# Spreading the hidden-dimension products of a Fourier layer over the blocks of a round

## The chip, the cores and the metric

The kernel runs on one core of one Trainium2 chip. The metric is the device time of one execution in microseconds (us). Work is done by TensorE (matmul, PE in the profile, its weight loads PEld), VectorE (DVE), ScalarE (ACT) and GpSimd (POOL); SyncE (SP) issues the DMA transfers.

## The reference

Four layers, on x of 2048 rows (S) and 640 columns (D), all in float32:

```python
x = x + A(layernorm(x))      # Fourier layer
x = x + B(layernorm(x))      # attention, causal window of 256, 32 heads of 20
x = x + A(layernorm(x))
x = x + B(layernorm(x))
# A(x): a = x @ dft_hid_re.T;  b = x @ dft_hid_im.T
#       y = dft_seq_re @ a - dft_seq_im @ b
```

The change lies in the Fourier layers A and at their last block. Float32 accuracy is reached with pairs of float16 numbers, a high and a low part, and three matmuls for each product (high by high, high by low, low by high).

## The kernel before

**Two Fourier layers and two attentions in turn.** The function `spectral` is a Fourier layer. The rows are 16 tiles of 128 (`NT`). Its work has two halves.

- A *stage* (`z_stage(s)`, from `Hidden.stage`) multiplies row tile s, normalised and transposed, by the hidden Fourier matrices (`whid`). It has four products of 15 matmuls, each into one of two `pf` PSUM banks. ACT empties a bank (L254), DVE empties it again with a subtraction (L257), and seven sums of the four results, split in high and low parts, go into a `zc` tile (L250 on ACT, L251 on POOL). A stage is 60 matmuls.
- A *block* (`main_a`, `main_b`, `main_c` for a round r and a pair j of output tiles) multiplies the sequence Fourier matrix by the `zc` tiles of one round. Seven products of 12 matmuls replace eight, in Strassen's manner, so the coefficients are sums too: `take_c` has POOL form them (L478 to L481), ACT round them to a high part (L486), and DVE form the low part (L489). A block is 84 matmuls, into the banks x, y and z, of which there are two each. DVE adds six of the seven results (L512) to residual rows or to slices of a scratch tile `pf`, and POOL adds three more (L526, L536, L547).

Four row tiles (`RS`) make a round, so a layer has four rounds (r = 0 to 3) of eight blocks (`NJ`, j = 0 to 7). The block's result is kept in the residual rows `res`, loaded ahead of the block and stored behind it: to `accd` in rounds 0 to 2, to `x2d` in the last.

**Where the stages stand before.** The four stages of round 0 come first. Of the stages for round r + 1, the first follows block 6 of round r, the second block 7, and the third and fourth stand at the start of round r + 1, ahead of its block 0. So blocks 0 to 6 run with no stage between them, and up to four stages come close together at the boundary. `zc` tiles have four buffers, beside two large `early` buffers that hold the tiles with s % 8 < 2.

**Side work.** `tick()` is called after each product of a stage and of a block (four times a stage, seven times a block). It pops one pair of coefficient roundings and advances every generator in the list `side` by a step. In the first Fourier layer the generators are: the norm of a row tile (`side_norm`, 11 steps from its load to the split tile `xs`), its transposes (`turn_x`, with a number of steps to wait first; `turned_x` ends it at once), the maxima of the attention's weights (`b_max`, DVE, L618, from round 0, block 1) and their splitting (`b_split`, ACT and POOL, L660 to L663, from round 1, block 2). Before, the norms for the next round begin ahead of blocks 3 and 4 and behind the transposes of the first two stages. In the second Fourier layer the normalised, transposed tiles were stored by the attention before it, and `hidden.fetch(s)` loads one into a ring of two; it stands just ahead of its stage.

**The last block.** In round 3, two tiles of the next attention are already prepared (`finish`, `ahead`). Ahead of block 7 two stacks are filled for that attention (`fill_stack`, eight loads each, tile `ks`), and the two residual rows of block 7 are loaded behind them by `main_a`. The attention's weights (`Projections`) take the large buffer that held the Fourier weights, once the last stage is over.

**What sets the order.** Each engine works through its own queue, and all loads and stores of this part are on SP's queue. The order in the source is not kept to the letter: in the trace six matmuls of the next block (`x<-early,cc`, at 143.49 us) stand between two products of a stage. `issue_after` holds some instructions behind others by hand.

Of the kernel before, what the change touches and what calls it, by code (L numbers as in the profile page):

```python
# [11 lines left out]
F32 = mybir.dt.float32  # L12
F16 = mybir.dt.float16
I32 = mybir.dt.int32
AF = mybir.ActivationFunctionType
OP = mybir.AluOpType
AX = mybir.AxisListType

S, D, H, DH, P = 2048, 640, 32, 20, 128
NT = S // P  # L20
ND = D // P
HD = D // 2
RS = 4
NR = NT // RS
NJ = NT // 2
# [24 lines left out]
TURN_STEPS = 8  # L50
NORM_STEPS = (4, 9)
ROW_STEPS = 3
X_UP = 2.0 ** 10
C_UP = 2.0 ** 8
W_UP = 2.0 ** 13
# [6 lines left out]
def body(ctx: ExitStack, tc: tile.TileContext, x_in, cmat, whid, wqkv, wo, out):  # L62
    nc = tc.nc
# [139 lines left out]
    class Hidden:  # L203
# [21 lines left out]
        def stage(self, s, pool, new=new_f):  # L225

            w, xt = self.w, self.xt(s)
            if s % 8 < 2:
                zc = new_early()[:, :14 * HD].rearrange("p (m a d) -> p m a d", m=7, a=2)
            else:  # L230
                zc = pool.tile([P, 7, 2, HD], F16, tag="zc", name="zc", bufs=4)
            self.zc[s] = zc
            b11, b12, t1, t2, t3, t4 = (self.zf[:, k] for k in range(6))
            z = None

            def product(c, n):
                nonlocal z
                z = new()
                cs = slice(n * HD, (n + 1) * HD)
                k = 0  # L240
                for dt in range(ND):
                    for l, r in ((0, 0), (0, 1), (1, 0)):
                        self.last = matmul(z[:, :HD], xt[:, l, dt], w[:, r, c, dt, cs],
                                                     start=k == 0, stop=k == 14).ins
                        k += 1
                        yield 136
                z = z[:, :HD]

            def parts(m, f):
                nc.scalar.activation(zc[:, m, 0], f, AF.Copy)  # L250
                nc.gpsimd.tensor_tensor(zc[:, m, 1], f, zc[:, m, 0], op=OP.subtract)  # L251

            def scaled(o):
                nc.scalar.activation(o, z, AF.Copy, scale=Z_DOWN)  # L254

            def minus(o, f):
                nc.vector.scalar_tensor_tensor(o, z, Z_DOWN, f, op0=OP.mult, op1=OP.subtract)  # L257

            yield from product(0, 0)
            scaled(zc[:, B11, 0])  # L260
            scaled(b11)
            minus(zc[:, B11, 1], zc[:, B11, 0])
            yield 0
            yield from product(0, 1)
            scaled(b12)
            minus(t1, b11)
            parts(T1, t1)
            yield 0
            yield from product(1, 1)
            scaled(zc[:, B22, 0])  # L270
            minus(t2, t1)
            minus(t3, b12)
            minus(zc[:, B22, 1], zc[:, B22, 0])
            parts(T2, t2)
            parts(T3, t3)
            yield 0
            yield from product(1, 0)
            scaled(zc[:, B21, 0])
            minus(zc[:, B21, 1], zc[:, B21, 0])
            minus(t4, t2)  # L280
            parts(T4, t4)
            yield 0
# [62 lines left out]
    def spectral(layer, res_src, hidden, first):  # L345
        with ExitStack() as st:
# [110 lines left out]
            def z_stage(s):  # L457
                for ns in hidden.stage(s, sb, spare if first and s < RS else new_f):
                    if ns == 0:
                        tick()  # L460
# [50 lines left out]
            def add(o, z, f):  # L511
                marks["dve"] = nc.vector.scalar_tensor_tensor(o, z, Y_DOWN, f, op0=OP.mult, op1=OP.add).ins  # L512
# [1 line left out]
            def new_bank(name):  # L514
                return pxy.tile([P, 512], F32, tag=name, name=name, bufs=2)

            def main_a(r, j):
                res = [keep.tile([P, D], F32, tag="res", name="res", bufs=4) for k in range(2)]
                for k in range(2):
                    load(res[k], res_src[2 * j + k] if r == 0 else acc_d[2 * j + k])  # L520
                f = sb.tile([P, 3, HD], F32, tag="pf", name="pf", bufs=2)
                x = new_bank("x")
                cc = CC.pop((r, j))
                z = product(r, x, cc, 0, True, False)
                marks["act"] = nc.scalar.activation(f[:, 0], z, AF.Copy, scale=Y_DOWN).ins
                nc.gpsimd.tensor_tensor(res[1][:, lo], res[1][:, lo], f[:, 0], op=OP.add)  # L526
                tick()
                state[r, j] = [res, f, cc, x]

            def main_b(r, j):  # L530
                (x0, x1), f, cc, x = state[r, j]
                p1, u2, u3 = (f[:, k] for k in range(3))
                y = new_bank("y")
                z = product(r, y, cc, 1, True, False)
                add(u2, z, p1)
                nc.gpsimd.tensor_tensor(x0[:, hi], x0[:, hi], u2, op=OP.add)  # L536
                tick()
                z = product(r, x, cc, 2, False, True)
                add(x0[:, lo], z, x0[:, lo])
                tick()  # L540
                zb = new_bank("z")
                z = product(r, zb, cc, 4, True, False)
                add(x1[:, hi], z, x1[:, hi])
                tick()
                z = product(r, y, cc, 3, False, False)
                add(u3, z, p1)
                nc.gpsimd.tensor_tensor(x1[:, hi], x1[:, hi], u3, op=OP.add)  # L547
                tick()
                state[r, j] = [(x0, x1), cc, y, zb]

# [121 lines left out]
            def keep_w():  # L672
                for k in range(2):
                    load(w_d[k], w[:, k].rearrange("p a b c -> p (a b c)"))
                    yield 1

            if first:
                constants()
                x = [load_x(s) for s in range(2)]
                f = [load_w(n) for n in range(NXIN - 2)]  # L680
                norm_x(0, x[:1], nc.vector)
                for n in range(10):
                    split_w(n, f[n])
                    if n == 1:
                        turn_x(0)
                        turned_x(0)
                        norm_x(1, x[1:], nc.gpsimd)
                    if n == 7:
                        x = [load_x(s) for s in range(2, 4)]
                    if n + NXIN - 2 < 10:  # L690
                        f.append(load_w(n + NXIN - 2))
            else:
                side.append(hidden.rest)
            load_c(0)
            for r in range(NR):
                for k in range(0 if r == 0 else 2, RS):
                    s = RS * r + k
                    if first:
                        if s == 1:
                            norm_x(2, x, nc.gpsimd)  # L700
                            marks["dve"] = normed[0]
                        if s:
                            turned_x(s)
                        if k < RS - 1:
                            turn_x(s + 1, 2)
                    elif s > 1:
                        hidden.fetch(s)
                    if r == 0 and k == 1:
                        load_c(1)
                        with behind() as order:  # L710
                            if not first:
                                order.enter_context(tc.issue_after(hidden.after))
                            take_c(0)
                    if first or s > 1:
                        z_stage(s)
                if r == NR - 1:
                    proj = Projections()
                for j in range(NJ):
# [9 lines left out]
                    if r == NR - 1 and j == NJ - 1:  # L728
                        for _ in early_qk:
                            pass  # L730
                        for k in (1, 0):
                            proj.stack[k] = new_stack()
                            fill_stack(proj.stack[k], 0, k)
                    if first:
                        if r < NR - 1 and j in (3, 4):
                            side.append(side_norm(RS * (r + 1) + j - 3))
                        if r < NR - 1 and j == 5:
                            turn_x(RS * (r + 1))
                    if j == 0 and r == 0:
                        with behind():  # L740
                            while splits:
# [4 lines left out]
                    with ExitStack() as order:  # L746
# [3 lines left out]
                        if j:  # L750
                            main_c(r, j - 1)
                        main_b(r, j)
                    if r < NR - 1 and j >= NJ - 2:
                        k = j - (NJ - 2)
                        s = RS * (r + 1) + k
                        if first:
                            turned_x(s)
                            turn_x(s + 1, 2 if k == 0 else 0)
                            side.append(side_norm(s + 2))
                        else:  # L760
                            hidden.fetch(s)
                        z_stage(s)
                main_c(r, NJ - 1)
                if r == NR - 1:
                    drain()
# [542 lines left out]
```

## Time and profile before

| | |
|---|---|
| runs | 2230.16, 2236.23, 2237.89 us |
| median of the runs | 2236.23 us |
| profiled execution, span from first to last instruction | 2233.0 us |
| median of the runs less that span | 3.2 us |
| PE, DVE, POOL, ACT busy | 2122.0, 1646.4, 1391.6, 1288.8 us |
| mean granted TensorE clock | 0.991 |

The profiled execution is told by its span; its time with what lies around the span is not listed apart, so the median stands for it. In a row of the timeline the first number is the start from the beginning of the span, the second the length, `x15` the number of instructions merged, and the brackets hold the engine's idle time before it and what ended that. The first Fourier layer runs from the start to about 591 us, the second from about 1174 to 1686 us; its first two stages already run inside the attention ahead of it.

### The profile page before, as it was taken

Reading aid. Unit: us, or ns where it says so; the run is one execution under the profiler, and the core shown is the slowest. Engines: PE = TensorE matmul, PEld = TensorE weight load, DVE = VectorE, ACT = ScalarE, POOL = GpSimd, SP = SyncE. Lnnn points to the kernel's source line nnn. Section 1 sums busy time; section 2 is a strip of 40 time slices with the busy share of each in tenths; the row PEclk is TensorE's granted clock in tenths of the full one; section 3 lists DMA queues with packets and bytes.
Section 4 is the critical chain, followed back from the end, with each engine's and each line's share of the span. In section 5 each row is a group of like instructions: output and inputs, shape, how many; then the busy total and the mean of one; then the engine's idle time right before and its main releaser. Section 6 shows DMA issues by size and latency. Waiting matters only on the chain.

```text
span 2233.0 us, 55112 instructions
## 1 busy us (share of the span) xinstructions
PE 2122.0 (95%) x21985; PEld 1494.7 (67%) x21985; DVE 1646.4 (74%) x3577; ACT 1288.8 (58%) x2155; POOL 1391.6 (62%) x1788
## 2 busy tenths in 40 slices
PE   7999899899999999999899999999998999999998
PEld 4767566676666766677566777777675666677765
DVE  8887958767677887887858758585767777777664
ACT  5434455443467777777754443434434777777775
POOL 5775968758355665566446858586674555566443
PEclk9999999999999999999999999999999999999999
DMA  6664646455533422333424536364743323332231
GB/s 252 219 224 143 229 138 225 156 188 175 142 79 67 103 71 73 94 91 84 134 79 160 193 127 212 110 207 145 256 133 96 83 63 85 93 87 59 57 80 37
DMA packets 187607, 292.96 MB, mean 131 GB/s; under 512 B 13908, under 2 KB 120660, under 8 KB 178004
## 3 DMA queue, kind: packets, MB, share of 16 engines
q1 hardware_dynamic: 186772, 288.77, 42.1%
q8 instruction: 172, 2.82, 0.5%
q14 instruction: 87, 0.71, 0.1%
q10 hardware_dynamic: 576, 0.66, 0.1%
HBM read 202.51 MB, written 86.87 MB: 130 GB/s over the span
## 4 chain that ended last, share of the span: by engine, by line
PE 59%; DVE 12%; DMA 4%; issue 3%; POOL 2%; ACT 2%; SPq 1%; DVEq 0%; POOLq 0%; ACTq 0%
PE pf L115 24%; PE pv L115 8%; PE y L115 7%; PE sp L115 5%; PE x L115 5%; PE z L115 5%; PE tp L115 3%; DVE m L1062 3%; DVE sp L1058 2%; PE pt L115 2%; DVE cc L489 1%; DMA res<-accd 1%; DMA x2d<-res 1%; PE acc L115 1%; DMA qs<-qkd 1%
## 5 line engine op out<-in xcount | busy, mean ns | idle before, releaser
L115 PEld LDWEIGHTS <-cc 128*128 128x128 f16 x5376 | 525.1, 98 | 215.6 <-issue 10.6
L1106 ACT ACTIVATE ptq<-tp,shift,alpha 128x768 f32<-128x768 f32 (+2 forms) x512 | 486.2, 950 | 163.6 <-PE tp L115 155.6
L115 PEld LDWEIGHTS <-big 128*128 128x128 f16 x4320 | 408.5, 98 | 151.9 <-issue 40.5
L1062 DVE TENSOR_REDUCE m<-sp 128x2 f32<-128x512 f32 (+1 forms) x512 | 345.1, 674 | 16.8
L1058 DVE COPY_PREDICATED sp<-mask,sp 128x256 f32<-128x256 int32 x448 | 190.8, 426 | 188.2 <-PE sp L115 176.5
L115 PE MATMUL pf<-early,big 128*128 128x256 f16 x2400 | 313.9, 274 | 2.9 <-ACT early L401 2.5
L1111 POOL TENSOR_SCALAR_AFFINE_SELECT ptq<-ptq 128x512 f32<-128x512 f32 x224 | 145.5, 649 | 265.4 <-ACT ptq L1106 261.7
L486 ACT ACTIVATE cc<-cs 128x512 f16<-128x512 f32 x256 | 151.6, 623 | 254.6 <-POOL cs L478 124.1
L115 PE MATMUL y<-zc,cc 128*128 128x320 f16 x1728 | 263.8, 300 | 2.4 <-DVE pf L512 2.4
L115 PE MATMUL pf<-big 128*128 128x320 f16 x1680 | 245.6, 304 | 19.2 <-DVE zc L257 9.3
L489 DVE SCALAR_TENSOR_TENSOR cc<-cs,cc 128x512 f16<-128x512 f32 x256 | 255.2, 1012 | 9.9 <-ACT cc L486 9.7
L489 DVE SCALAR_TENSOR_TENSOR cc<-cq,cc 128x512 f16<-128x512 f32 x192 | 198.7, 1036 | 0.0
L1113 POOL TENSOR_SCALAR_AFFINE_SELECT ptq<-ptq 128x512 f32<-128x512 f32 x256 | 163.9, 640 | 43.1 <-ACT ptq L1106 43.1
L115 PE MATMUL pv<-ptq,v 128*32 128x128 f32 (+1 forms) x3840 | 183.7, 330 | 0.0
L115 PE MATMUL z<-zc,cc 128*128 128x320 f16 x1152 | 178.5, 299 | 2.0 <-ACT cc L486 1.0
L115 PE MATMUL x<-zc,cc 128*128 128x320 f16 x1152 | 179.7, 299 | 0.0
L115 PE MATMUL sp<-ks,qs 62*128 62x256 f16 (+1 forms) x1792 | 153.6, 248 | 20.8 <-DVE m L1062 18.6
L115 PE MATMUL pf<-big,early 128*128 128x320 f16 x960 | 162.3, 301 | 6.4 <-DVE x L883 6.4
L1083 ACT ACTIVATE qs<-pt 2x512 f16<-2x512 f16 x224 | 131.0, 585 | 42.7 <-PE pt L115 40.0
L115 PE MATMUL tp<-qs,ks 62*128 62x128 f16 x2688 | 150.1, 217 | 3.2 <-ACT ptq L1106 2.7
L115 PE MATMUL pf<-bo,ot 128*128 128x320 f16 x840 | 147.2, 302 | 3.3 <-DVE ot L956 2.8
L167 POOL TENSOR_TENSOR xs<-lny,xs 128x640 f16<-128x640 f32 x63 | 94.2, 1497 | 83.3 <-ACT xs L166 82.6
(144 smaller groups left out, 3525.3 us busy)
## 6 DMA issues: line engine op xcount, KB each, us to landing
cq<-in_cmat_dram SPq DMA_DIRECT2D x64, 1024.0 KB
accd<-res SPq DMA_DIRECT2D x96, 320.0 KB
res<-accd SPq DMA_DIRECT2D x96, 320.0 KB
x<-x2d SPq DMA_DIRECT2D x64, 320.0 KB
qkd<-early SPq DMA_DIRECT2D x160, 128.0 KB
ks<-qkd SPq DMA_DIRECT2D x108, 160.0 KB
qs<-qkd SPq DMA_DIRECT2D x84, 160.0 KB
x2d<-res SPq DMA_DIRECT2D x32, 320.0 KB
```

What stands on the lines that cost most here:

```text
L115: i = getattr(nc.tensor, what)(*args, **kw)
L167: eng.tensor_tensor(lo, y, hi, op=OP.subtract)
L486: nc.scalar.activation(cc[m][:, 0], f, AF.Copy, scale=C_UP)
L489: nc.vector.scalar_tensor_tensor(cc[m][:, 1], f, C_UP, cc[m][:, 0], op0=OP.mult, op1=OP.subtract)
L1058: nc.vector.copy_predicated(sp[:, :, 2 * P:3 * P], mask[:, None, :].to_broadcast([P, 2, P]), far)
L1062: topped[0] = nc.vector.tensor_reduce(TOP[g // 4][:, g % 4], sp[:, :, c0:3 * P], axis=AX.X, op=OP.max).ins
L1083: nc.scalar.activation(o, handed[n][rs].rearrange("r (i p) t -> r i p t", i=2), AF.Copy)
L1106: nc.scalar.activation(q[:, h:h + 2, a0 + first:a0 + 3], tp[:, :, first * P:3 * P].rearrange("p a (b c) -> p a b c", c=P), AF.Sigmoid, bia ...
L1111: nc.gpsimd.affine_select(out=q[:, :, a0], in_=q[:, :, a0], pattern=[[0, 4], [-1, P]], base=0, channel_multiplier=1, compare_op=OP.is_gt, ...
L1113: ins = nc.gpsimd.affine_select(out=q[:, :, a0 + 2], in_=q[:, :, a0 + 2], pattern=[[0, 4], [1, P]], base=0, channel_multiplier=-1, compare ...
```

## The change

- The stages of the next round stand behind blocks 2, 4, 5 and 6 in round 0, and behind blocks 1, 3, 5 and 6 in rounds 1 and 2 (`STAGES`). None is left at the start of a round but the first.
- In the first Fourier layer each stage's norm begins three blocks ahead of it (`starts`), which for the first stage of rounds 2 and 3 is in the round before; its transposes wait four steps from the block ahead of the stage, or two from the end of the previous stage's.
- In the second Fourier layer the fetch of tile s + 2 stands right behind stage s.
- `zc` gets six buffers instead of four. The room comes from a slice of the scratch tile `pf` (its third sum is written over the first) and from a smaller DMA scratch.
- The residual rows of the last block are loaded ahead of the two stacks.

```diff
+STAGES = ((2, 4, 5, 6), (1, 3, 5, 6), (1, 3, 5, 6))
...
-                zc = pool.tile([P, 7, 2, HD], F16, tag="zc", name="zc", bufs=4)
+                zc = pool.tile([P, 7, 2, HD], F16, tag="zc", name="zc", bufs=6)
...
+            RES = {}
+
+            def load_res(r, j):
                 res = [keep.tile([P, D], F32, tag="res", name="res", bufs=4) for k in range(2)]
                 for k in range(2):
                     load(res[k], res_src[2 * j + k] if r == 0 else acc_d[2 * j + k])
-                f = sb.tile([P, 3, HD], F32, tag="pf", name="pf", bufs=2)
+                return res
+
+            def main_a(r, j):
+                res = RES.pop((r, j), None) or load_res(r, j)
+                f = sb.tile([P, 2, HD], F32, tag="pf", name="pf", bufs=2)
...
-                add(u3, z, p1)
-                nc.gpsimd.tensor_tensor(x1[:, hi], x1[:, hi], u3, op=OP.add)
+                add(p1, z, p1)
+                nc.gpsimd.tensor_tensor(x1[:, hi], x1[:, hi], p1, op=OP.add)
...
+            def starts(k):
+                return [max(NJ * r + STAGES[r][k] - 3, k) for r in range(NR - 1)]
...
-                for k in range(0 if r == 0 else 2, RS):
+                for k in range(RS if r == 0 else 0):
...
                     if first or s > 1:
                         z_stage(s)
+                    if not first and s > 1:
+                        hidden.fetch(s + 2)
...
+                        RES[r, j] = load_res(r, j)
                         for k in (1, 0):
                             proj.stack[k] = new_stack()
                             fill_stack(proj.stack[k], 0, k)
                     if first:
-                        if r < NR - 1 and j in (3, 4):
-                            side.append(side_norm(RS * (r + 1) + j - 3))
-                        if r < NR - 1 and j == 5:
-                            turn_x(RS * (r + 1))
+                        for k in range(RS):
+                            if n in starts(k):
+                                side.append(side_norm(RS * (starts(k).index(n) + 1) + k))
+                        if r < NR - 1 and j == STAGES[r][0] - 1:
+                            turn_x(RS * (r + 1), 4)
...
-                    if r < NR - 1 and j >= NJ - 2:
-                        k = j - (NJ - 2)
+                    if r < NR - 1 and j in STAGES[r]:
+                        k = STAGES[r].index(j)
                         s = RS * (r + 1) + k
                         if first:
                             turned_x(s)
-                            turn_x(s + 1, 2 if k == 0 else 0)
-                            side.append(side_norm(s + 2))
-                        else:
-                            hidden.fetch(s)
+                            if k < RS - 1:
+                                turn_x(s + 1, 2)
                         z_stage(s)
+                        if not first and s + 2 < NT:
+                            hidden.fetch(s + 2)
...
-    nc = _bacc.Bacc("TRN2", target_bir_lowering=False, num_devices=1)
+    nc = _bacc.Bacc("TRN2", target_bir_lowering=False, num_devices=1, dynamic_dma_scratch_size=1024)
```

More of the change, by code (lines that the diff above doesn't have):

```diff
@@ L515, in new_bank @@
                 return pxy.tile([P, 512], F32, tag=name, name=name, bufs=2)
-            def main_a(r, j):
+            RES = {}
+            def load_res(r, j):
                 res = [keep.tile([P, D], F32, tag="res", name="res", bufs=4) for k in range(2)]
@@ L531, in main_b @@
                 (x0, x1), f, cc, x = state[r, j]
-                p1, u2, u3 = (f[:, k] for k in range(3))
+                p1, u2 = (f[:, k] for k in range(2))
                 y = new_bank("y")
```

## The prediction

> **What bounds the kernel now.** I read the page first, then a table of stretches of the two Fourier layers, then TensorE's timeline around the stretches that lose time, and last all engines around one such place.
>
> From the page:
>
> ```profile
> PE 2122.0 (95%) x21985; PEld 1494.7 (67%) x21985; DVE 1646.4 (74%) x3577; ACT 1288.8 (58%) x2155; POOL 1391.6 (62%) x1788
> ```
>
> TensorE is the bound, but a share over the whole span doesn't say where the missing time lies. So I cut the first Fourier layer (54 to 592 us) at the round boundaries, and set beside it two stretches of the second Fourier layer, which runs the same loop. The columns are the stretch, its length, busy time and instructions of PE, PEld, DVE, ACT and POOL, the granted TensorE clock and the DMA load:
>
> ```profile
> core 0: us, PE busy (x) PEld busy (x) DVE busy (x) ACT busy (x) POOL busy (x), PEclk, DMA share, GB/s
> 54.00:130.00 76.00, 74.45 (x553) 53.46 (x551) 67.83 (x116) 31.90 (x59) 60.26 (x46) 1.00 0.66 221
> 130.00:166.00 36.00, 32.12 (x235) 22.60 (x234) 28.14 (x56) 14.60 (x30) 25.80 (x21) 0.95 0.63 214
> 166.00:247.00 81.00, 79.88 (x595) 57.18 (x592) 63.39 (x128) 37.36 (x73) 54.31 (x45) 1.00 0.49 163
> 247.00:308.00 61.00, 50.35 (x355) 35.33 (x356) 43.77 (x71) 31.92 (x58) 54.07 (x41) 0.92 0.60 202
> 308.00:389.00 81.00, 80.48 (x599) 57.69 (x597) 62.59 (x114) 41.09 (x78) 58.49 (x48) 1.00 0.57 189
> 389.00:426.00 37.00, 28.68 (x195) 19.47 (x196) 29.85 (x41) 14.31 (x27) 34.02 (x25) 0.93 0.56 183
> ...
> 1206.00:1268.00 62.00, 62.00 (x463) 44.76 (x461) 54.53 (x74) 23.79 (x44) 53.60 (x39) 1.00 0.64 222
> 1268.00:1326.00 58.00, 57.89 (x427) 41.57 (x425) 30.82 (x58) 25.23 (x55) 34.56 (x34) 1.00 0.36 119
> ```
>
> Inside a round of the first layer PE is almost never idle (81.00 - 79.88 and 81.00 - 80.48). At the three boundaries it loses 3.88, 10.65 and 8.32 us, 22.85 in all, and the granted clock falls to 0.92 to 0.95. The second layer's boundary (1268 to 1326) loses 0.11 us. So what the spreading of the stages can win lies in the first layer alone, at three places. TensorE's timeline names the waits there (start, length, instruction, count, and in brackets the idle time before it and its releaser):
>
> ```profile
> 139.79 3.25 PE L115 MATMUL pf<-big 128*128 128x320 f16 x15 [2.61 <-DVE zc L257]
> ...
> 162.40 2.20 PE L115 MATMUL pf<-big 128*128 128x320 f16 x15 [1.27 <-DVE zc L257]
> ...
> 248.36 0.45 PE L115 MATMUL pf<-idh,xs 128*128 128x128 f16 x5 [2.48 <-POOL xs L167]
> ...
> 279.77 4.16 PE L115 MATMUL pf<-big 128*128 128x320 f16 x15 [7.32 <-DVE early L257]
> ...
> 285.16 2.20 PE L115 MATMUL pf<-big 128*128 128x320 f16 x15
> ...
> 303.74 3.35 PE L115 MATMUL pf<-big 128*128 128x320 f16 x15 [1.97 <-DVE early L257]
> ...
> 390.33 0.45 PE L115 MATMUL pf<-idh,xs 128*128 128x128 f16 x5 [1.85 <-POOL xs L167]
> ...
> 422.02 4.16 PE L115 MATMUL pf<-big 128*128 128x320 f16 x15 [5.26 <-DVE zc L257]
> ...
> 457.36 4.44 PE L115 MATMUL pf<-big 128*128 128x320 f16 x30 [0.19 <-DVE zc L257]
> ```
>
> Three kinds. Twice the transposes of the next rows wait for their norm (xs from POOL): 2.48 + 1.85 = 4.33 us. Three times the third product of the stage after block 6 waits until DVE has emptied a pf bank: 2.61 + 7.32 + 5.26 = 15.19 us. Three times a product of a later stage waits likewise: 1.27 + 1.97 + 0.19 = 3.43 us. After such waits 15 matmuls take 3.25, 4.16, 3.35 and 4.16 us, where the undisturbed 15 at 285.16 take 2.20: slow tails of 1.05 + 1.96 + 1.15 + 1.96 = 6.12 us. Together 29.07 us.
>
> Why DVE is late, from all engines ahead of the wait at 422:
>
> ```profile
> 414.95 1.15 ACT L486 ACTIVATE cc<-cs 128x512 f16<-128x512 f32 x2 [2.72 <-POOL cs L479]
> 415.00 1.60 POOL L481 TENSOR_TENSOR cs<-cq,cs 128x512 f32<-128x512 f32 x1
> 415.79 3.89 DVE L489 SCALAR_TENSOR_TENSOR cc<-cs,cc 128x512 f16<-128x512 f32 x3
> ...
> 417.69 0.42 ACT L254 ACTIVATE zc<-pf 128x320 f16<-128x320 f32 x1
> ...
> 421.49 0.48 DVE L257 SCALAR_TENSOR_TENSOR zc<-pf,zc 128x320 f16<-128x320 f32 x1
> ```
>
> The stage's first eviction stands on ACT behind the high parts of the next block's coefficients, which wait for POOL's sums, and on DVE behind their low parts (3.89 us for three). These engines lag behind PE when the stage comes, and two pf banks cover no more. The second layer has the same queues without the norms and the weight splitting:
>
> ```profile
> 1272.48 8.58 PE L115 MATMUL pf<-big 128*128 128x320 f16 x60
> 1276.29 0.48 DVE L257 SCALAR_TENSOR_TENSOR zc<-pf,zc 128x320 f16<-128x320 f32 x1
> ...
> 1281.09 0.32 SPq L175 DMA_DIRECT2D big<-xud  x1
> ...
> 1303.72 16.49 PE L115 MATMUL pf<-big 128*128 128x320 f16 x120
> ```
>
> There DVE frees the first bank at 1276.29 + 0.48 = 1276.77, and the third product is due at half of 8.58 us, about 1276.8: no stall, but no margin either. Two stages in a row there (120 matmuls, 16.49 us) run without a gap.
>
> **The change part by part.** Instruction counts on every engine stay: 12 stages, 12 norms, 12 row loads in the first layer, 14 fetches in the second. What moves is where they stand.
>
> *Transposes.* A norm takes 11 ticks (4 to load, 7 to work), a block gives 7 and a stage 4, and norms now begin three blocks ahead of their stage, with the transposes a block or more later. The 4.33 us go; cover is a whole block of 84 matmuls, and if it were gone the 4.33 come back. I take -4.3.
>
> *Later stages at the boundary.* With a main block between any two stages there are 7 products between their evictions, so the 3.43 us of waits go. -3.4. Their load on the queues doesn't vanish, and is counted in the next term.
>
> *The stage behind a run of blocks.* Before, 7 blocks run without a stage; after, at most 3 (7, 0, 1 or 0 to 2), then 2 or 1. What makes DVE, ACT and POOL late in the first layer (operations between 54 and 426 us, with count, busy time and mean ns; the last row is from the view of one source line and has min, median and max ns):
>
> ```profile
> L663 POOL TENSOR_TENSOR bst<-wst,bst 128x640 f16<-128x640 f32 x15 | 24.1, 1609 | 2.6 <-ACT bst L661 2.6
> L618 DVE TENSOR_REDUCE wmax<-wst 128x1 f32<-128x640 f32 x20 | 16.2, 808 | 0.7 <-DMA wst<-in_wo_dram 0.7
> L251 POOL TENSOR_TENSOR zc<-big,zc 128x320 f16<-128x320 f32 x28 | 22.3, 812 | 21.8 <-ACT zc L250 21.8
> L257 DVE SCALAR_TENSOR_TENSOR big<-pf,big 128x320 f32<-128x320 f32 x33 | 15.2, 482 | 16.6 <-ACT big L254 5.8 <-ACT zc L254 5.6 <-ACT early L254 5.2
> ...
> L489 DVE SCALAR_TENSOR_TENSOR cc<-cs,cc x92: 675/1102/1889, 60.9 to 418.3; 128x512 f16<-128x512 f32 x92
> ```
>
> The worst lag, 7.32 us over 7 blocks, is 1.05 a block. A stage gives time back: 60 matmuls are 8.2 us of PE (half of 16.49), against 8 DVE operations of 0.482 (3.9 us) and 4 on POOL of 0.812 (3.2 us), over 4 us each time. By that, runs of 3 blocks (3.1 us) are repaid before the next and all 15.19 us go. Against it: the extra work isn't even. The maxima of the weights (20 of 0.808) and all four norms of the first round now meet in blocks 0 to 3, and the split of the weights (15 of 1.609 on POOL) meets norms in both later rounds; and the second layer shows that base lag alone uses the cover up. If the lag is only paid in smaller portions, none of it goes. Ends -15.2 and 0; nothing is nearer to either, so half, -7.6.
>
> *Slow tails.* They hang on the stalls: ends -6.1 and 0, half is -3.1. The rows show a slow tail after a wait of 2.61 and 1.97 us too, not after 1.27. [...]
>
> *Last round.* It had two stages directly ahead of its block 0 and now has block 7 there. Waits of PE in it, first layer:
>
> ```profile
> 504.49 1.79 PE L115 MATMUL z<-zc,cc 128*128 128x320 f16 x12 [1.00 <-ACT cc L486]
> ...
> 506.89 3.42 PE L115 MATMUL y<-zc,cc 128*128 128x320 f16 x24 [0.61 <-DVE pf L512]
> ...
> 528.98 2.52 PE L115 MATMUL pf<-early,big 128*128 128x256 f16 x15 [2.52 <-ACT early L401]
> ```
>
> That is 4.13 us. Without the relief they may double; since the attention's weights can load once the last stage is over, now a block earlier, they may vanish. Ends -4.1 and +4.1 per layer; I take +1 each, +2 in both, since the run of blocks without a stage grows by one.
>
> *Residual rows of the last block.* Their two loads now stand ahead of sixteen stack loads on SP:
>
> ```profile
> 578.77 2.05 SPq L175 DMA_DIRECT2D res<-accd  x2
> ...
> 584.74 1.79 PE L115 MATMUL y<-zc,cc 128*128 128x320 f16 x12 [0.58 <-DVE pf L512]
> ...
> 587.49 0.86 POOL L536 TENSOR_TENSOR res<-res,pf 128x320 f32<-128x320 f32 x1 [14.00 <-DMA res<-accd]
> ...
> 588.78 1.79 PE L115 MATMUL z<-zc,cc 128*128 128x320 f16 x12 [0.21 <-DVE res L512]
> ```
>
> POOL waits 14.00 us for them, which looks large, but PE loses only 0.21 of it: the 0.58 at 584.74 is one product waiting for the bank that DVE just read, which the load doesn't touch. The stacks land about 2.05 us later; all are issued by 578.77 and first read when the attention starts, after the product at 588.78. So -0.2 per layer, -0.4 in both (ends -0.8 for the whole wait with what follows, and +2).
>
> *The rest at nothing.* The third pf slice goes because the last sum is written over p1; DVE's write waits for POOL's read of p1, which is three products older. If that cover were gone, one y bank would be held longer. The DMA issue list has SP's queues alone, so nothing in it shows a use of the smaller scratch. In the second layer the fetch at 1281.09 already leaves as the stage ends (1272.48 + 8.58 = 1281.06), more than 20 us ahead of the stage that needs it (1303.72): writing it behind the stage changes nothing, and SP's wait for that slot is there already, with PE never held.
>
> Sum: -4.3 - 3.4 - 7.6 - 3.1 + 2.0 - 0.4 = -16.8 us. The profiled execution spans 2233.0 us, so 2216.2; the median of the runs is 2236.2, 3.2 above that span, so 2219.4.
>
> **The rivals.**
>
> *All lags repaid.* The 15.2 and 6.1 go whole and the last round loses nothing: -4.3 - 3.4 - 15.2 - 6.1 - 0.4 = -29.4, 2206.8 us. For it: the balance of 4 us a stage against 1.05 a block. Against: bunched norms.
>
> *The lag is paid in portions, or the order hardly moves.* Every stage then waits a little, 15.2 and 6.1 stay: -4.3 - 3.4 + 2.0 - 0.4 = -6.1, 2230.1 us. For it: the second layer's margin of nothing.
>
> *Slower: each of the first layer's 12 stages finds DVE late.* The six waits for a pf bank average 18.62 / 6 = 3.1 us, with 6.12 / 6 = 1.0 of tail. Paid at all 12 stages that is 49 us in place of 24.7, so +24.7 - 4.3 + 2.0 - 0.4 = +22, 2258 us. It decides from a mean loss of 2.3 us a stage, at which the sum is zero. For it: the low part of a coefficient takes 675 ns at best and 1889 at worst, and stages now put POOL work beside twice as many of them. [...] Against: the second layer does it after block 6 with no stall.
>
> **How the numbers follow.** The forecast (2211 to 2227) gets 0.46, the full repayment 0.23, the portions 0.15, the slower case 0.16. Under 0.3% (6.7 us) a measurement of this kernel tells little, its three runs lying 7.7 us apart. So faster 0.69, same 0.15, slower 0.16. The range runs from just below the full repayment, 2204, to the lighter part of the slower case, 2240.
>
> **What would show it.** Right: in the first layer no transposes waiting for POOL xs, no wait over 4 us ahead of a stage's third product, granted clock near 1.00 at the boundaries; the second layer's Fourier loop unchanged within 2 us; POOL's 14 us wait for res gone with PE's end of block moved by a few tenths. Wrong: waits for DVE at most of the 12 stages, summing over 25 us; new gaps in the second layer's mid-round stages; or longer gaps in the last round.

## The result and the profile after

| | before | changed |
|---|---|---|
| median of six runs | 2232.52 us | 2217.49 us |
| lowest to highest | 2230.16 to 2237.89 | 2212.66 to 2221.21 |
| profiled execution, span | 2233.0 us | 2219.4 us |

The ratio is 0.9932, 95% interval 0.9917 to 0.9947: 15 us faster. The profiled execution of the changed kernel took 2221.21 us, 1.8 us more than its span, and was the slowest of its six.

The page of the changed kernel, the first line of its first part:

```profile
PE 2115.5 (95%) x21985; PEld 1493.1 (67%) x21985; DVE 1615.9 (73%) x3577; ACT 1283.3 (58%) x2155; POOL 1376.1 (62%) x1788
```

PE has the same 21985 instructions and 6.5 us less of busy time. The stretches of the first Fourier layer, of the first attention and of the second Fourier layer, with the columns as before (the granted clock is the third number from the end):

```profile
54.00:578.00 524.00, 498.20 (x3734) 360.00 (x3731) 382.19 (x734) 231.95 (x446) 380.70 (x330) 0.99 0.55 190
578.00:1163.00 585.00, 554.77 (x7256) 383.61 (x7255) 454.49 (x1182) 424.86 (x649) 320.94 (x566) 0.99 0.33 89
1163.00:1673.00 510.00, 502.88 (x3738) 363.15 (x3737) 341.42 (x588) 200.59 (x406) 353.05 (x314) 1.00 0.50 173
```

The first layer is counted here from its first block to the first product of the attention. For the kernel before the same count runs from 53.75 to 591.15:

```profile
54.00:592.00 538.00, 506.01 (x3740) 362.71 (x3738) 401.74 (x735) 235.68 (x447) 389.25 (x330) 0.98 0.56 185
```

So the first layer went from 537.4 to 524.4 us (53.74 to 578.11), 13.0 less; PE's idle time fell by some 6 us and its busy time by some 7, at a granted clock of 0.99 in place of 0.98. The first attention took 585.2 after 584.6, the second layer 509.7 after 509.9, the second attention 546.4 after 547.4. The gain lies in the first Fourier layer, as forecast. Its waits in the changed kernel, from TensorE's timeline:

```profile
74.45 0.45 PE L116 MATMUL pf<-idh,xs 128*128 128x128 f16 x5 [2.62 <-ACT xs L167]
...
94.46 2.20 PE L116 MATMUL pf<-big 128*128 128x320 f16 x15 [2.03 <-DVE zc L258]
...
98.90 2.20 PE L116 MATMUL pf<-big 128*128 128x320 f16 x15 [0.84 <-ACT big L402]
...
128.92 2.20 PE L116 MATMUL pf<-big 128*128 128x320 f16 x15 [1.74 <-DVE zc L258]
...
214.40 2.20 PE L116 MATMUL pf<-big 128*128 128x320 f16 x15 [1.45 <-DVE early L258]
...
241.93 1.79 PE L116 MATMUL y<-zc,cc 128*128 128x320 f16 x12 [1.24 <-DVE pf L513]
...
252.17 4.16 PE L116 MATMUL pf<-big 128*128 128x320 f16 x15 [4.38 <-DVE early L258]
...
308.22 4.37 PE L116 MATMUL pf<-big 128*128 128x320 f16 x30 [1.67 <-DVE zc L258]
...
354.98 3.20 PE L116 MATMUL pf<-big 128*128 128x320 f16 x15 [3.52 <-DVE zc L258]
...
389.76 2.20 PE L116 MATMUL pf<-big 128*128 128x320 f16 x15 [1.43 <-DVE zc L258]
```

The waits for a pf bank held by DVE are 2.03 + 1.74 + 1.45 + 4.38 + 1.67 + 3.52 + 1.43 = 16.22 us. They were 18.62, so almost all are still there. But they come in seven pieces with a maximum of 4.38 in place of 7.32, and only two have a slow tail (15 matmuls in 4.16 and 3.20, not 2.20). Last round and last block, same view:

```profile
494.89 1.79 PE L116 MATMUL z<-zc,cc 128*128 128x320 f16 x12 [1.04 <-ACT cc L487]
...
498.28 3.42 PE L116 MATMUL y<-zc,cc 128*128 128x320 f16 x24 [1.59 <-DVE pf L513]
...
512.00 0.45 PE L116 MATMUL pf<-idh,xs 128*128 128x128 f16 x5 [1.87 <-POOL xs L168]
...
572.72 1.79 PE L116 MATMUL z<-zc,cc 128*128 128x320 f16 x12
...
575.98 2.20 PE L116 MATMUL pf<-big,early 128*128 128x320 f16 x15
```

In the last round 1.04 + 1.59 + 1.87 = 4.50 us against 4.13 in the rows of before. At the block's end no product waits.

### The profile page after: what moved, and what is told of

It reads as the page before. It is cut to its first block, busy times and chain, and to the rows that moved or that the text cites. A ratio compares the mean times of both kernels' runs of the same rounds, so it can differ in the third digit from the quotient of the medians.

```text
span 2219.4 us, 55110 instructions
## 1 busy us (share of the span) xinstructions
PE 2115.5 (95%) x21985; PEld 1493.1 (67%) x21985; DVE 1615.9 (73%) x3577; ACT 1283.3 (58%) x2155; POOL 1376.1 (62%) x1788
## 4 chain that ended last, share of the span: by engine, by line
PE 72%; DVE 17%; issue 4%; DMA 3%; ACT 2%; POOL 2%; SPq 0%; DVEq 0%; POOLq 0%; ACTq 0%
PE pf L116 27%; PE y L116 11%; PE pv L116 8%; PE x L116 8%; PE z L116 7%; PE sp L116 5%; DVE cc L490 4%; PE tp L116 3%; DVE m L1076 3%; DVE sp L1072 2%; PE pt L116 2%; DMA res<-accd 1%; DVE lnt L141 1%; DMA qs<-qkd 1%; PE acc L116 1%
## 5 line engine op out<-in xcount | busy, mean ns | idle before, releaser
L116 PEld LDWEIGHTS <-cc 128*128 128x128 f16 x5376 | 524.4, 98 | 213.2 <-issue 10.0
L1076 DVE TENSOR_REDUCE m<-sp 128x2 f32<-128x512 f32 (+1 forms) x512 | 345.2, 674 | 16.8
L490 DVE SCALAR_TENSOR_TENSOR cc<-cs,cc 128x512 f16<-128x512 f32 x256 | 228.6, 901 | 0.0
L554 POOL TENSOR_TENSOR res<-res,pf 128x320 f32<-128x320 f32 x64 | 77.2, 1206 | 136.4 <-DVE pf L513 123.8
```

The source lines that it names most:

```text
L116: i = getattr(nc.tensor, what)(*args, **kw)
L490: nc.vector.scalar_tensor_tensor(cc[m][:, 1], f, C_UP, cc[m][:, 0], op0=OP.mult, op1=OP.subtract)
L554: nc.gpsimd.tensor_tensor(x1[:, hi], x1[:, hi], p1, op=OP.add)
L1076: topped[0] = nc.vector.tensor_reduce(TOP[g // 4][:, g % 4], sp[:, :, c0:3 * P], axis=AX.X, op=OP.max).ins
```

## The experiments

All ratios are to the kernel before on the same chip; its medians there were 2232.67, 2233.57 and 2232.95 us in the three sets of runs.

**The residual rows alone.** The kernel before, with

```diff
...
+                        RES[r, j] = load_res(r, j)
                         for k in (1, 0):
                             proj.stack[k] = new_stack()
...
```

> The kernel before with the last block's residual rows ahead of the stacks, and nothing else of the change. Theory: the two block ends, where PE waited 1.37 us in the first layer (565 to 592) and 1.16 us in the second (1660 to 1686), lose all of it, so about 2.5 us under the kernel before: 2230.0 beside 2232.5. Rival, the term as it was predicted: 0.4 us, 2232.1; the waits then stay in the trace and went with the moved stages.

Measured: 2227.55 us, ratio 0.9978 (0.9969 to 0.9987), 5 us less. The products at both block ends wait no more; the first layer took 534.7 us (2.7 less) and the second 508.0 (1.9 less). The theory holds for the waits, and the predicted 0.4 was too small: the waits of 0.58 us at each end, which I took to be untouched, went too. The time fell by about twice the 2.5 us that these waits come to (by 2.9 to 6.9, by the interval); where the rest comes from is not shown. The price that the prediction allowed for does show: one of the attention's first products waits 0.78 us for its stack (589.48), which it did not before.

**Without the residual rows.** The changed kernel less that line.

> The changed kernel with the residual rows behind the stacks again. Theory: POOL waits some 14 us for res again and PE loses 2.5 us at the two block ends: 2220.0 beside 2217.5. Rival: 0.4 us, 2217.9.

Measured: 2230.72 us, ratio 0.9994 (0.9983 to 1.0005): without this line the whole change wins nothing that can be told. Both theories fall. At the end of the first layer:

```profile
567.05 1.29 SPq L176 DMA_DIRECT2D res<-accd  x2
...
574.12 0.86 POOL L543 TENSOR_TENSOR res<-res,pf 128x320 f32<-128x320 f32 x1 [13.57 <-DMA res<-accd]
...
574.94 0.86 POOL L533 TENSOR_TENSOR res<-res,pf 128x320 f32<-128x320 f32 x1
575.41 3.36 PE L116 MATMUL z<-zc,cc 128*128 128x320 f16 x12 [4.24 <-DVE res L513]
575.83 0.49 DVE L513 SCALAR_TENSOR_TENSOR pf<-y,pf 128x320 f32<-128x320 f32 x1
...
578.56 3.13 PE L116 MATMUL y<-zc,cc 128*128 128x320 f16 x12
```

PE waits 4.24 us ahead of the z product, and its 12 matmuls then take 3.36 us in place of 1.79; in the second layer it is 4.35 and 3.36. The kernel before waited only 0.21 there, with the same late rows (POOL waited 14.00 us then, 13.57 now). The last lines show what is new. DVE writes its sum into pf (575.83) only behind POOL's addition at 574.94, which reads p1. POOL can't read p1 before the residual rows are there, DVE can't write over it before POOL has read it, and the y bank stays taken, so the y product stands behind the z product, at 578.56. In the kernel before, DVE wrote the third slice at 584.20 and let the y bank go while POOL still waited, so a y product (584.74) and 15 matmuls of the attention ran ahead of the z product at 588.78 and covered its wait:

```profile
584.20 0.49 DVE L512 SCALAR_TENSOR_TENSOR pf<-y,pf 128x320 f32<-128x320 f32 x1 [4.84 <-PE y L115]
...
586.37 2.20 PE L115 MATMUL pf<-big,early 128*128 128x320 f16 x15
```

The small edit, and not the moved stages, was the next suspect.

**The write over p1 alone.** The kernel before, with

```diff
...
-                p1, u2, u3 = (f[:, k] for k in range(3))
+                p1, u2 = (f[:, k] for k in range(2))
...
-                add(u3, z, p1)
-                nc.gpsimd.tensor_tensor(x1[:, hi], x1[:, hi], u3, op=OP.add)
+                add(p1, z, p1)
+                nc.gpsimd.tensor_tensor(x1[:, hi], x1[:, hi], p1, op=OP.add)
```

> The kernel before with the third sum written over p1 and two pf slices, nothing else of the change. Theory: at the last block POOL reads p1 only when the residual rows are there, so DVE can't write over it, the y bank stays taken and PE waits at both block ends, some 4 to 5 us each: 2241 beside 2232.5. Rival, as predicted: the write over p1 costs nothing, 2232.5.

Measured: 2241.69 us, ratio 1.0032 (1.0021 to 1.0043), 8 us slower. At the two block ends:

```profile
589.21 3.36 PE L115 MATMUL z<-zc,cc 128*128 128x320 f16 x12 [5.10 <-DVE res L512]
...
1686.48 3.21 PE L115 MATMUL z<-zc,cc 128*128 128x320 f16 x12 [5.18 <-DVE res L512]
```

These waits of 5.10 and 5.18 us and the slow matmuls behind them, less the waits that the kernel before had there, come to 10.7 us. In this profile the two Fourier layers took 5.8 and 5.3 us more than before, so the block ends account for the loss.

**Both small edits, no stage moved.** The two diffs above together.

> The kernel before with the write over p1 and the residual rows ahead: both small edits, no stage moved. Theory: the early rows give POOL its read of p1 in time, so the 8 us that the write over p1 costs alone go whole, and the time is that of the residual rows alone, 2227.5 beside 2232.7. Rival: the write over p1 costs by itself and the two add up, -5 + 8: 2236.

Measured: 2228.77 us, ratio 0.9984 (0.9970 to 0.9998). The cost of the write over p1 is gone once the rows are early, within what these intervals can tell, and no product waits at either block end. So the small edits are worth about 4 us together, and the moved stages, with their norms and the six `zc` buffers, bring the ratio from 0.9984 to 0.9932, about 11.5 us. The first layer took 536.7 us here and 524.4 in the changed kernel.

**The second layer alone.** The changed kernel, with the first layer's stages, norms and transposes in their old places:

```diff
...
-                    if r < NR - 1 and j in STAGES[r]:
-                        k = STAGES[r].index(j)
+                    at = (NJ - 2, NJ - 1) if first else STAGES[min(r, NR - 2)]
+                    if r < NR - 1 and j in at:
+                        k = at.index(j)
...
```

> The changed kernel with the first layer's stages, norms and transposes where they were before; the second layer's stages stay spread and the residual rows stay ahead. Theory: the second layer had no stalls to win back, so only the block ends remain, less up to 1.6 us in the second layer's last round: 2230 to 2232 beside 2232.5, with the first layer's stalls of 2.6, 7.3 and 5.3 us back. Rival: the second layer or the order of the attentions carries the gain, 2222 or less.

Measured: 2230.96 us, ratio 0.9992 (0.9981 to 1.0002). The first layer is back at 537.6 us, with waits of 2.62, 6.02 and 5.27 at the three stages. The theory holds. The six `zc` buffers are there in this run too, so they alone don't shorten the first layer. Norms and transposes move with their stages in every run here; what each is worth by itself is not told apart.

**The first layer alone.** The counterpart, the second layer's stages in their old places (its fetches stay as changed).

> The changed kernel with the second layer's stages where they were before, the first layer's spread. Theory: the second layer wins nothing by the spread and pays some 1.6 us in its last round, so this is 1 to 2 us under the changed kernel, 2215.5 to 2216.5. Rival: the spread pays in the second layer too, over 2219.

Measured: 2217.62 us, ratio 0.9940 (0.9924 to 0.9956), not to be told from the changed kernel. In its profile the second layer took 508.7 us against 509.7, and its last round waits 0.89 and 0.61 us where the changed kernel waits 1.05 and 1.59. The sign is the expected one; the size lies below what these runs resolve.

**More lag, before.** The kernel before with POOL's subtraction in the weight splitting made twice:

```diff
                     nc.gpsimd.tensor_tensor(lo, f, hi, op=OP.subtract)
+                    nc.gpsimd.tensor_tensor(lo, f, hi, op=OP.subtract)
```

> The kernel before with POOL's subtraction in the weight splitting (15 of 1.6 us, in rounds 1 and 2 of the first layer) made twice, the second time over the same result: 24 us more of POOL. Theory: this lag is paid at the stage behind the run of seven blocks, so the boundaries of rounds 1 and 2 lose more: 8 to 16 us slower, 2241 to 2249 beside 2232.5. Rival: POOL's lag doesn't set the stalls (DVE's own does): within 3 us of the kernel before.

Measured: 2257.14 us, ratio 1.0102 (1.0084 to 1.0120), 23.6 us slower: all of the added POOL time, more than expected.

```profile
254.68 0.72 PE L115 MATMUL pf<-idh,xs 128*128 128x128 f16 x5 [5.90 <-POOL xs L167]
...
278.99 1.79 PE L115 MATMUL y<-zc,cc 128*128 128x320 f16 x12 [3.00 <-DVE pf L512]
...
295.89 4.16 PE L115 MATMUL pf<-big 128*128 128x320 f16 x15 [11.04 <-DVE early L257]
...
322.01 3.78 PE L115 MATMUL pf<-big 128*128 128x320 f16 x15 [3.43 <-DVE early L257]
```

The wait at the stage behind the long run is 11.04 us (7.32 before), and the lag now shows ahead of it too, at the transposes (5.90) and a block's y bank (3.00).

**More lag, after.** The same doubling in the changed kernel.

> The changed kernel with the same doubled subtraction. Theory: each stage gives time back before the next, so the added 24 us of POOL cost the changed kernel less than half of what they cost the kernel before: 3 to 6 us, 2221 to 2224 beside 2217.5. Rival, the lag paid in portions: the same cost in both kernels, whatever its size.

Measured: 2224.04 us, ratio 0.9950 (0.9932 to 0.9968), 4 us by the ratios and 6.5 us by the medians more than the changed kernel. Its largest wait is 4.91 us (4.38 without the doubling):

```profile
253.54 4.16 PE L116 MATMUL pf<-big 128*128 128x320 f16 x15 [4.91 <-DVE early L258]
```

The same 24 us of work cost the kernel before some four to six times as much; in the profiles the first layer is 24.1 us longer there and 3.2 us here. So a stage between the blocks does let POOL catch up, and lag doesn't pile up over a round.

**Stages between blocks, but late.**

```diff
-STAGES = ((2, 4, 5, 6), (1, 3, 5, 6), (1, 3, 5, 6))
+STAGES = ((4, 5, 6, 7), (4, 5, 6, 7), (4, 5, 6, 7))
```

> The changed kernel with the stages behind blocks 4, 5, 6 and 7 of every round: none at the start of a round, but one run of four blocks (0 to 3) without a stage. Theory: what counts is that a main block stands between any two stages, and a run of four is little worse than one of three: 2216 to 2221 beside 2217.5. Rival: the even spread is what pays, and half of the first layer's 13 us comes back: 2224.

Measured: 2228.04 us, ratio 0.9966 (0.9955 to 0.9977). The rival holds: half of the gain or a little more is lost. In the profile the first layer took 531.5 us, against 524.4 in the changed kernel.

```profile
119.62 4.16 PE L116 MATMUL pf<-big 128*128 128x320 f16 x15 [4.62 <-DVE zc L258]
...
258.18 3.60 PE L116 MATMUL pf<-big 128*128 128x320 f16 x15 [6.65 <-DVE early L258]
...
377.79 1.76 PE L116 MATMUL z<-early,cc 128*128 128x320 f16 x6 [5.23 <-DVE res L513]
...
398.19 3.57 PE L116 MATMUL pf<-big 128*128 128x320 f16 x15 [5.05 <-DVE zc L258]
```

Behind the runs of blocks 0 to 4 the waits are 4.62, 6.65 and 5.05 us again, as large as those of before (2.61, 7.32 and 5.26), and a block's z product waits 5.23 us inside such a run. Block 4 ends a run of five, not four as the expectation had it, since the stage stands behind it. What pays is a short run, not only a block between two stages.

**Four banks behind a stage.** The changed kernel, with

```diff
+            def other():
+                turn[0] += 1
+                return new_bank("x") if turn[0] % 2 else new_f()
...
-                for ns in hidden.stage(s, sb, spare if first and s < RS else new_f):
+                for ns in hidden.stage(s, sb, spare if first and s < RS else other):
```

> The changed kernel with the products of every stage but the first round's going in turn to an x bank and a pf bank, so that four banks stand behind a stage in place of two. Theory: the waits of the stages are for banks, and DVE and ACT catch up within a stage, so the 16.2 us of waits for a pf bank in the first layer and their slow tails of 3.1 us go: about 2199 beside 2217.5 of the changed kernel. Rival: DVE is late for good, and the wait moves to the next block's x, y and z banks: 2214 to 2219.

Measured: 2204.32 us, ratio 0.9874 (0.9861 to 0.9887), 13 us under the changed kernel. That is two thirds of what the theory claimed. In the profile the first layer took 514.7 us, 9.7 less, where the theory had all 19.3 of its waits and tails go. The waits that remain:

```profile
98.22 3.08 PE L116 MATMUL pf<-big 128*128 128x320 f16 x15 [1.96 <-DVE big L258]
...
251.29 4.16 PE L116 MATMUL pf<-big 128*128 128x320 f16 x15 [4.25 <-DVE big L258]
...
350.11 2.20 PE L116 MATMUL pf<-big 128*128 128x320 f16 x15 [1.60 <-DVE big L258]
...
382.78 2.20 PE L116 MATMUL pf<-big 128*128 128x320 f16 x15 [0.98 <-DVE big L258]
```

Four waits of 1.96, 4.25, 1.60 and 0.98 us are left of seven, and at the next blocks' banks none over 0.5 us came up. The waits for a bank fell from 16.22 to 8.79 us. So about half of what the spread left was for want of banks, and it didn't move to the blocks. What the other half hangs on is not shown: the bank is now let go by a subtraction that DVE writes into the scratch of the stage (`big`), which none of these edits touches.

**A combined version.** The four banks in the first layer, the second layer in its old places, the weight splitting begun at block 1 with six ticks of pause in place of five, and the first transposes of round 1 five ticks later.

> The version that the runs point to: x banks beside pf for the first layer's stages, second layer as before, the weight splitting begun a block earlier and with one more tick between its pieces, the first transposes of round 1 five ticks later. Theory: against the kernel with x banks alone (2204.3) 1.6 us less in the second layer, 2.6 us less at the first transposes, and part of the 4.3 us wait of the second stage of round 2: 2196 to 2201. Rival: the splitting only moves its load onto other stages: 2201 to 2205.

Measured: 2200.81 us, ratio 0.9864 (0.9845 to 0.9883), the fastest of all, and within its forecast. Against the four banks alone the intervals overlap, so what the later edits add is not settled; in the trace the transposes' wait of 2.62 us is gone, and the wait of 4.25 us is 1.78, but the first stage's of 1.96 has become 3.45 and one of 1.77 us has come at 213. Its stages' waits come to 8.98 us in all, no less than with the four banks alone.

## Why the prediction was right, and where its steps were not

The time (2217.5 against 2219.4), the sign and the place (the first layer's three boundaries) were right. The sum was -16.8 us, the medians say -15.0 and the profiled executions -13.6. That the sum came so close is in part luck. The two terms for transposes and stages were 12.2 us too large together, and 5.9 us came from where the sum had less or nothing. The forecast also started from 2236.23 us, the median of three runs, which is 3.7 above the median of six. Term by term, by the traces:

| term | forecast | measured |
|---|---|---|
| transposes waiting for their norm | -4.3 | -0.7 |
| later stages, and the stage behind a run | -3.4 - 7.6 | -2.4 |
| slow tails | -3.1 | -3.2 |
| last round, both layers | +2.0 | +1.9 |
| residual rows of the last block | -0.4 | -2.5 |
| waits of blocks for their own banks | not in the sum | -2.0 |
| slow clock in the last round | not in the sum | -1.8 |

*Transposes.* The step that failed is "cover is a whole block". The two old waits went, but the first norm of round 0 begins at block 0 and can't begin earlier, and its transposes came due in block 1 (2.62 us at 74.45): the seven steps of block 0 and the four of waiting are just the norm's own eleven, so there was no cover at all. With five steps more, in the combined version, this wait is gone. Two more short waits, 0.84 at 98.90 and 0.17, are for pf banks that hold transposes.

*Stages.* I took half of 15.19 between two ends, on the thought that lag repaid means no wait. The mechanism was right: doubled POOL work costs 24 us before and 4 to 6 after. The size was not: 16.22 us stayed. The step that failed is "so the 3.43 us of waits go" with half of the 15.19: a stage still waits behind a run of one to three blocks (1.43 to 4.38 us at seven of the 12). About half of what stayed was for want of banks, and four banks took 10 us more out of the first layer. That the rest comes from the stage's own place in the queues is argued, not shown. The remark that the second layer's base lag alone uses the cover up was the better guide. What the spread won from the waits was their peaks: the slow tails and the blocks' own waits (0.36 + 1.02 + 0.17 + 0.51 + 0.57 + 0.65 = 3.28 us before, 1.24 after).

*Clock in the last round.* From 530 to 565 it was 0.95 and is 1.00 (35 us by 0.05). The row of 15 matmuls in 2.52 us behind the 2.52 us wait was quoted in the prediction, but its slow clock was not costed: the undisturbed 15 at 533.91 took 1.80 us, and the 12 at 531.29 took 2.78 where those at 535.55 took 1.79. With the rows alone the wait is there too (2.65 us at 528.06, then 2.87 and 2.43 us), as with the second layer alone (2.61 us at 530.78, then 3.23 and 2.08 us); the changed kernel and the first layer alone have no such wait. What takes it away was not isolated.

*Residual rows and p1.* "The rest at nothing" failed outright, in the one place that the prediction named as cover: POOL's read of p1 is three products older, but at the last block POOL stands still for 14 us. That edit alone costs 8 us; the early rows take it away. The prediction costed the two edits one by one, and each by the old trace: the rows at -0.4 and p1 at 0. Alone they are -5 and +8, together -4. The changed kernel less the early rows is as slow as the kernel before. Had the change left them out, the same sum would have given 2219.8 us, 11 below the 2230.7 measured.

*Last round and second layer* came out as costed: 2.93 us of waits in the second layer's last round are 4.50 now, and 0.4 us came on top in the first layer's. All bank waits of the second layer's stages together are 0.23 us.

*The rivals.* The portions were half right: the waits did stay, yet 2230 was wrong, since their tails and the blocks' waits went. The slower case didn't come: the mean loss at a first layer's stage is 16.22 / 12 = 1.4 us, with 0.25 of tail, below the 2.3 that it needed. No run here isolates what POOL's work does to the low parts that the rival drew on; between 54 and 426 us their row went from 675/1102/1889 ns (min, median, max) to 641/683/1911 in the changed kernel.

The terms sum to -10.7 us; some 3 us of the profiled difference lie in pieces that were not assigned. The second attention is 1.0 us of it and slow matmuls a little behind the tails are another 0.7; the rest stays open. The first attention is no part of it (584.6 and 585.2 us), but it shows how far a single profile can be trusted: the change doesn't touch it, and it took from 578.4 to 585.2 us in the profiles of the kernels here that begin the second layer in the same order. The granted clock was 0.94 in its last 84 us in the longest, the changed kernel's, and 0.98 to 1.00 in every stretch from 580 to 1150 us with the second layer alone, where it took 579.9 us.

*The signs named in advance.* POOL's 14 us wait went, and the second layer stayed within 2 us. But one transposes' wait of 2.62 us, released by ACT, and one stage's wait of 4.38 us are there, so the boundaries were less clean than the term for them said. Of the signs of being wrong, longer waits in the last round came, by 1.9 us in both layers, as their own term had it; waits for DVE were at 7 of the 12 stages and summed to 16.22 us, not over 25.

## What to carry to other kernels

Spreading a burst of work over a loop paid here (about 11.5 us) because other engines fell behind in the loop and PE had to wait for them at the burst (7.32 us behind seven blocks); a test is to double the suspected lag in both versions and compare what it costs (23.6 us against 4 to 6.5). Much of what the burst waited for stayed with it where it was put, 16.22 us of 18.62; here two more banks took about half of that, and another place did not. When a scratch slice is saved by writing over an operand, look for every reader of that operand on other engines at the place where that engine waits longest (here 14.00 us, and the edit alone cost 8 us), not in the steady state.

## What the runs showed of the hardware that I had not expected

In these profiles the slow tail behind a wait of PE is not settled by the length of the wait between about 2 and 3.5 us. The same wait for the first stage's third product took 2.61 us in the profile of the kernel before, 2.60 with the residual rows ahead and 2.62 with the second layer alone; the 15 matmuls behind it took 3.25, 3.71 and 2.20 us:

```profile
139.79 3.71 PE L115 MATMUL pf<-big 128*128 128x320 f16 x15 [2.60 <-DVE zc L257]
```

```profile
139.64 2.20 PE L116 MATMUL pf<-big 128*128 128x320 f16 x15 [2.62 <-DVE zc L258]
...
145.40 3.78 PE L116 MATMUL pf<-big 128*128 128x320 f16 x15 [0.17 <-ACT big L402]
```

In the second of these the slow matmuls came later, behind a further wait of 2.15 us of the transposes at 143.98, so a full-speed row right behind a wait doesn't mean that the wait was free. At 355 us a wait of 3.52 us was followed by 15 matmuls in 3.20 us in the changed kernel, and one of 3.51 by 2.20 without the residual rows:

```profile
354.60 2.20 PE L116 MATMUL pf<-big 128*128 128x320 f16 x15 [3.51 <-DVE zc L258]
```

The stages' waits over 4 us in the first layer's rows (4.05 to 11.04 us) all had a tail, and those below 1.9 us, but for the one at 145.40, had next to none (at most 30 matmuls in 4.45 us, where an undisturbed 30 took 4.24). At 2 us both came: a wait of 1.97 us and then 15 matmuls in 3.35 us in the kernel before, and one of 2.03 us and then 15 in 2.20 in the changed kernel. What decides between them is not shown. In the changed kernel's profile the five waits from 1.43 to 2.03 us had next to no tail (at most 0.13 us), and the two longest, 4.38 and 3.52 us, had tails of 1.96 and 1.00 us. The term came to -3.2, not to its end of -6.1, because these two tails stayed, 2.96 us of the 6.12.
